# A linear-attention layer and its feed-forward net on one core: w_in fetched for two weight groups at a time

## The chip, the core and the metric

The kernel runs on one core of a Trainium2 chip. A core has a matrix engine (TensorE, PE in the profile), which also loads its stationary operands (PEld), a vector engine (VectorE, DVE), a scalar engine (ScalarE, ACT), a general one (GpSimd, POOL) and SyncE (SP), which here does nothing but issue transfers. Each engine works through its own list of instructions in a fixed order and waits at semaphores. Sixteen DMA engines move data between the memory of the chip and the 128 partitions of the on-chip buffer. The metric is the device time of one execution in microseconds (us).

## What is computed

```python
def _attn_ref(r, k, v, w, u):          # r, k, v, w: (4, 8, 768, 48), u: (8, 48)
    state = zeros((B, H, D, D))
    for t in range(S):
        cur = einsum('bhd,bhe->bhde', u[None] * k[:, :, t], v[:, :, t])
        y[:, :, t] = einsum('bhd,bhde->bhe', r[:, :, t], state + cur)
        state = w[:, :, t, :, None] * state + einsum('bhd,bhe->bhde', k[:, :, t], v[:, :, t])

def _moe_ref(x, w_in, w_out):          # x: (3072, 384), w_in: (384, 2048), w_out: (2048, 384)
    h = maximum(x @ w_in, 0.0)
    return (h * h @ w_out).astype(float32)
```

The attention's output, laid out as 3072 tokens of 384 channels, is the x of the feed-forward net. The inputs r, k, v, w and u are 4-byte floats. The weights w_in and w_out come as 8-byte floats, so a row of w_in has 16 KB and a row of w_out 3 KB.

## The kernel before

**Tiling.** The sequence of 768 steps is cut into six chunks of 128. Chunk c of sequence b (four sequences) is one attention unit; its output goes, transposed, into the tile x, 128 tokens of each sequence, so that a chunk gives the feed-forward net 512 tokens. That net runs over 16 blocks f of 128 hidden channels: `first` (L569, matmuls of L573) makes the block's hidden values in a PSUM tile hp, lines 578 to 582 on ACT and DVE apply the squared relu and split it into a rounded part and a rest (tile g), and `second` (L585, matmuls of L588) adds the block's share to the output tile ob. For the first chunk the blocks f 0 to 5 are done in halves of two sequences each (`HALF`, L605), 12 half blocks; from f = 6 on a block takes all 512 tokens.

**Weights.** They lie in eight groups g; group g holds the blocks 2g and 2g + 1. `load_w` (L298) issues for each group four transfers of w_in into the tile ri (for each half j of the partitions one of 48 partitions with three pieces of 2 KB each, 288 KB, and one of 16 partitions with three pieces, 96 KB; L305) and one of w_out into ro (768 KB, L307). In w_in a piece is 256 channels of 8 bytes out of a row of 16 KB. `split_w` (L310) then turns each group's w_in, and each group's w_out, into two 4-byte parts: on ACT a widening read into a buffer q (L318), on DVE three passes over q (L322, L326, L331), on ACT the rounded part (L338), on POOL the rest (L339). There are two buffers q. The results wi and wo lie where the raw data lay.

**Attention loads.** For chunk 1 and later, w, k and r of two sequences go by three transfers into a tile st (L358); DVE transposes blocks of it (L367); 16 transfers on chip spread these into the tile pt (L377); then the scans (L411) begin.

**Order.** The order of all instructions is written down before the program runs, by the class Plan. Every step is added with an engine, a cost, a rank and what it reads and writes. `order` (L75) keeps a clock for each engine and repeatedly takes, over all engines, the step that can start first; among those that can start at the same time on an engine, the one of lowest rank. For SP it models the transfers: at most eight in flight (`LANES`, L46, and the program waits likewise: each transfer waits for the semaphore of the eighth before it), a limit on the pieces outstanding (`RUNS`), and a result counts as there some time after the data has passed (`SLACK`). The ranks that matter here, from the tables of L598 to L604: a group's loads have W0[g] + WL[g], which is -20.75, -17.5, -10, -5.25, -1.5, -1.5, -3.25 and 3.5 for the groups 0 to 7; its splits have W0[g], -12.5, -9.5, -1, 0.25, 0.25, 5.5, 5.0 and 17. The st loads of chunk 1, first two sequences, have -7.25 and the 16 spreads after them -5.25. ro of group 6 shares its place with small tiles of chunk 0 and can be loaded only after these are read (L299); ri of group 7 likewise waits for a tile of the first loads.

So SP issues, in this order, ri and ro of the groups 0 and 1 among the loads of chunk 0; ri and ro of group 2; st of chunk 1 (three transfers); ri and ro of group 3; ri of group 6; ri of group 4; the 16 spreads; ro of groups 6 and 4; ri and ro of group 5; a v; ri and ro of group 7.

Of the kernel before, what the change touches and what calls it, by code (L numbers as in the profile page):

```python
# [10 lines left out]
F32R = mybir.dt.float32r  # L11
U8 = mybir.dt.uint8
U32 = mybir.dt.uint32
# [156 lines left out]

@with_exitstack
def kernel(
    ctx: ExitStack,
# [18 lines left out]
    R = 2 * D  # L194
    J = 64
    HP = J + D
    NF = DF // 128
    KT = DM // 128
    NG = NF // 2


    placed = {}

    def place(name, shape, dtype, at):
        n = 1
# [18 lines left out]
    for i in range(3):  # L224
        g = place(f"g{i}", [128, 2, 512], F32R, None)
# [11 lines left out]
    far = const.tile([128, NC * B], F32, name="far")  # L237
# [17 lines left out]
    P = Plan()  # L255
# [34 lines left out]
    w_in32 = w_in.bitcast(U32).rearrange("r (g x) -> g r x", g=NG)  # L290
    w_out32 = w_out.bitcast(U32).rearrange("(g f p) x -> g p f x", p=128, f=2)
    wi = {2 * g + f: wi_t[g].rearrange("p z (k f x) -> p z k f x", k=KT, f=2)[:, :, :, f] for g in range(NG) for f in range(2)}
    wo = {2 * g + f: wo_t[g][:, :, f * DM:f * DM + DM] for g in range(NG) for f in range(2)}

    def first_use(n):
        return [s for s in P.steps if both[n]["st"] in s.slots]

    def load_w(g, rank):  # L298
        before = first_use(0) if g == NG - 1 else [s for s in P.steps if any(x.pool == "ly" for x in s.slots)] if g == NG - 2 else []  # L299

        pairs = w_in32[g, 0:KT * R].rearrange("(k p) x -> p k x", k=KT)
        for j in range(2):
            last = w_in32[g, KT * R + j * D:KT * R + j * D + D].rearrange("(k p) x -> p k x", k=KT)
            for i, (to, n, src) in enumerate(((j * J, D, pairs[j * D:j * D + D]), (j * J + D, J - D, last))):
                P.add("sp", 1.4 if n == D else 0.5, rank, lambda to=to, n=n, src=src: nc.sync.dma_start(out=wi_r[g][to:to + n], in_=src),  # L305
                      w=[("wi", g, j, i)], after=before if g == NG - 1 else [], runs=3 * n)
        P.add("sp", 2.4, rank, lambda: nc.sync.dma_start(out=wo_r[g], in_=w_out32[g]), w=[("wo", g, 0, 0)],  # L307
              after=before, runs=256)

    def split_w(g, rank):  # L310
        for nm, rt, tt, parts in (("wi", wi_r[g], wi_t[g], [("wi", g, j, i) for j in range(2) for i in range(2)]),
                                  ("wo", wo_r[g], wo_t[g], [("wo", g, 0, 0)])):
            bits = rt.rearrange("p k x -> p (k x)").rearrange("p (x z) -> p x z", z=2)
            q = Slot("q")
            raw, lead = (nm, g, "raw"), (nm, g, "lead")

            def widen(q=q, bits=bits):
                A.activation(q.tile, bits.bitcast(F32)[:, :, 1], AF.Copy, scale=2.0 ** -112)  # L318
# [19 lines left out]
            P.add("act", 0.74, rank, lambda q=q, tt=tt: A.copy(out=tt[:, 0], in_=q.tile), r=[q], w=parts + [lead])  # L338
            P.add("pool", 1.9, rank, lambda q=q, tt=tt: G.tensor_tensor(out=tt[:, 1], in0=q.tile, in1=tt[:, 0].bitcast(F32), op=ALU.subtract),  # L339
                  r=[q, lead], w=[(nm, g, "rest")])  # L340
# [257 lines left out]
    AT = {"load": -12.5, "z": -10, "pt": -10.5, "rk": -7.0, "beta": -5.0, "far": 9.25, "v": -6.0, "scan": -2.25, "ln": 7.0, "rt": -6, "kn": 3.25, "diag": -3.5, "mt": 5, "mask": 3.25, "ktp": 5.25, "kt": 12.5, "mix": 4.25, "x": 1.5, "x3": -5.0, "send": 3.0, "dS": 3.5, "S": 1.25}  # L598
    AT0 = {"load": -13.0, "turn": -1.5, "rk": -2, "beta": 0.2, "far": 9.25, "v": -6.75, "scan": -1.75, "ln": 5.25, "rt": 0.25, "kn": 2, "diag": 9.5, "mt": -1.0, "mask": 3.75, "ktp": 7.25, "kt": -1, "mix": 3, "x": 7.75, "x3": -1, "send": 4.0, "dS": 7.5, "S": -4}
    U0 = (-16, -15.25, -6.75, -5.5)  # L600
    C1 = (5.25, 13, 34.5, 36)
    WL = (-8.25, -8, -9, -5.5, -1.75, -7, -8.25, -13.5)
    OFF = {"hp": -1.0, "g": -6.5, "ob": 0.75, "os": -7.5}
    W0 = (-12.5, -9.5, -1, 0.25, 0.25, 5.5, 5.0, 17)  # L604
    HALF = (6, 16, 0, 0, 0, 0)  # L605
    LAG = 2

    def rank_of(c, b):
        if c == 0:
            return lambda nm: U0[b] + AT0[nm]  # L610
        return lambda nm: (C1[b] if c == 1 else 8 * ((c - 1) * B + b) - 4) + AT[nm]

    for b in range(B):
        attention(0, b, rank_of(0, b))
    for g in range(NG):
        load_w(g, W0[g] + WL[g])
        split_w(g, W0[g])
    x = 0
    for c in range(NC):
        if c:  # L620
            for b in range(B):
                attention(c, b, rank_of(c, b))

        order = [(f, bs) for bs in ((0, 2), (2, B)) for f in range(HALF[c])] + [(f, (0, B)) for f in range(HALF[c], NF)]
        for f, bs in order:
            step = (bs[1] - bs[0]) / 2
            ffn(P, c, f, lambda nm, x=x, step=step: x + OFF[nm] + (LAG * step if nm in ("ob", "os") else 0), bs)
            x += step
    with tc.manual_schedule():
        P.run()  # L630
# [14 lines left out]
    with tc.If(any_bad > 0):  # L645
        with tc.tile_pool(name="dram", bufs=1, space=bass.MemoryType.DRAM) as dr, \
# [8 lines left out]
            with tc.For_i(0, S, TB) as t0:  # L655
# [8 lines left out]
                for t in range(TB):  # L664
                    rt, kt, wt = (tk[nm][:, t].unsqueeze(2).broadcast_to(sh) for nm in "rkw")
# [7 lines left out]
                for b in range(B):  # L673
                    nc.sync.dma_start(
                        out=xd[b * S:b * S + S].rearrange("s (h d) -> h s d", d=D)[:, ds(t0, TB)],
                        in_=ys[b * H:b * H + H])
            with tc.For_i(0, S, C) as s0:
# [17 lines left out]
                P = Plan()  # L695
# [36 lines left out]
```

## Time and profile before

| | |
|---|---|
| time, median of 3 runs | 560.74 us (558.96 to 561.72) |
| span of the profiled execution | 559.9 us |
| PE busy | 530.8 us, 95% of the span |
| DVE busy | 359.1 us, 64% |
| ACT busy | 288.0 us, 51% |
| POOL busy | 101.3 us, 18% |
| transfers issued from SP (q1) | 49.17 MB, 43.9% of 16 engines |
| w_in transfers of 288 KB, 16 of them, median to landing | 9.1 us |
| w_in transfers of 96 KB, 16 of them | 8.1 us |
| w_out transfers of 768 KB, 8 of them | 9.6 us |

Shares of busy time are over the whole span. The span has two parts: about 110 us in which the weights arrive and are split while the first two chunks run, and the rest, in which only PE has no idle time. The page gives no own time for the profiled execution beside its span; the median of the runs is 0.8 us above the span.

### The profile page before, as it was taken

The page shows a single profiled execution, that of the slowest core. Times are in us where ns is not written, and L with a number is a line of the kernel's source. Part 1 is how long each engine was busy: PE and PEld are TensorE (multiplying, and loading weights), DVE is VectorE, ACT ScalarE, POOL GpSimd, SP SyncE. Part 2 cuts the span into 40 slices and gives each one's busy share as a digit, 9 for nine tenths or more (in the row PEclk, how much of TensorE's full clock was granted, in tenths as well). Part 3 has the DMA queues.
Part 4 walks back from the last instruction along what each step waited for, and adds up shares of the span by engine and source line. Part 5 has one row for each costly group of instructions (what it writes and reads, how often), then busy time and mean ns, then how long its engine had stood idle before and what let it go on. Part 6 is the DMA issues. An engine that isn't in the chain of part 4 may idle for free. (4 is left out here: it accounts for less than half of the span.)

```text
span 559.9 us, 10076 instructions
## 1 busy us (share of the span) xinstructions
PE 530.8 (95%) x3800; PEld 466.7 (83%) x3800; DVE 359.1 (64%) x643; ACT 288.0 (51%) x677; POOL 101.3 (18%) x115
## 2 busy tenths in 40 slices
PE   4768898999999999999999999999999999999995
PEld 3557787889998999988888888888888888998994
DVE  5789879898759596776866767567475233332330
ACT  2786776668554747555554554553563222332322
POOL 4253552352203003030401102102000000000000
PEclk9998898999999999999999999999999999999999
DMA  9999699237472645637470470460440000010001
GB/s 156 210 240 217 122 255 218 39 64 137 99 141 51 111 109 91 123 78 135 80 132 2 78 168 24 84 129 2 78 106 3 12 1 1 14 58 2 0 1 60
DMA packets 206326, 50.86 MB, mean 91 GB/s; under 512 B 196032, under 2 KB 201152, under 8 KB 206272
## 3 DMA queue, kind: packets, MB, share of 16 engines
q1 hardware_dynamic: 205552, 49.17, 43.9%
q10 hardware_dynamic: 720, 0.98, 0.5%
q8 instruction: 32, 0.52, 0.4%
q14 instruction: 22, 0.18, 0.1%
HBM read 31.65 MB, written 4.72 MB: 65 GB/s over the span
## 5 line engine op out<-in xcount | busy, mean ns | idle before, releaser
L573 PE MATMUL hp<-x,wi 128*128 128x512 f32 (+1 forms) x1062 | 225.6, 358 | 4.7 <-DVE g L582 4.7
L588 PE MATMUL ob<-wo,g 128*128 128x384 f32 x1152 | 224.7, 341 | 4.4 <-ACT g L581 4.4
L588 PEld LDWEIGHTS ob<-wo,g 128*128 128x128 f32 x1152 | 200.5, 189 | 12.2 <-ACT g L581 4.9
L573 PEld LDWEIGHTS hp<-x,wi 128*128 128x128 f32 x1062 | 175.5, 190 | 31.9 <-DVE g L582 5.8
L579 DVE SCALAR_TENSOR_TENSOR hp<-hp,t 128x512 f32<-128x512 f32 (+1 forms) x118 | 70.2, 596 | 110.5 <-ACT t L578 110.0
L578 ACT ACTIVATE t<-hp 128x512 f32<-128x512 f32 (+1 forms) x118 | 60.9, 516 | 136.8 <-PE hp L573 111.2
L582 DVE TENSOR_TENSOR g<-hp,g 128x512 fp32r<-128x512 f32 (+1 forms) x118 | 69.1, 586 | 37.7 <-ACT g L581 35.9
L581 ACT CAST g<-hp 128x512 fp32r<-128x512 f32 (+1 forms) x118 | 59.2, 504 | 54.6 <-DVE hp L579 54.4
L448 ACT ACTIVATE m<-ident,beta 128x128 f32<-128x128 f32 x192 | 60.5, 395 | 7.0 <-DVE beta L441 7.0
L438 POOL TENSOR_TENSOR st<-st 128x384 f32<-128x384 f32 x24 | 25.1, 1047 | 64.7 <-DVE st L367 63.5
L463 DVE COPY_PREDICATED m<-caus,a 128x512 f32<-128x512 uint8 x48 | 33.0, 731 | 5.5 <-PE a L459 5.5
L459 PEld LDWEIGHTS a<-pt 48*128 48x128 f32 x384 | 25.8, 199 | 11.4 <-issue 7.1
L459 PE MATMUL a<-pt 48*128 48x128 f32 x384 | 30.8, 298 | 4.4 <-DVE pt L431 4.4
L526 DVE SCALAR_TENSOR_TENSOR x<-a,x 112x128 fp32r<-112x128 f32 (+2 forms) x44 | 17.9, 432 | 20.5 <-ACT x L525 19.9
L493 PE MATMUL a<-m,v 128*48 128x128 f32 (+1 forms) x384 | 28.5, 291 | 2.3 <-DVE m L463 1.8
L525 ACT ACTIVATE x<-a 112x128 fp32r<-112x128 f32 (+2 forms) x44 | 15.2, 389 | 28.8 <-PE a L493 28.5
L411 DVE TENSOR_TENSOR_SCAN pt<-pt,zero 112x128 f32<-112x128 f32 x80 | 28.9, 410 | 0.3 <-DMA x<-x 0.3
L493 PEld LDWEIGHTS a<-m,v 128*48 128x48 f32 (+1 forms) x384 | 21.4, 134 | 7.5 <-issue 4.5
L440 POOL TENSOR_TENSOR st<-st,un 128x384 f32<-128x384 f32 x24 | 26.9, 1120 | 1.6
L367 DVE STREAM_TRANSPOSE st<-st 128x1152 f32<-128x1152 f32 x20 | 26.8, 1359 | 0.0
L553 POOL TENSOR_TENSOR S<-S,Ec 112x192 f32<-112x192 f32 x16 | 8.2, 510 | 102.0 <-DVE S L552 102.0
L418 ACT ACTIVATE m<-pt 112x512 f32<-112x512 f32 x24 | 15.2, 635 | 20.1 <-DVE pt L411 15.7
(72 smaller groups left out, 394.5 us busy)
## 6 DMA issues: line engine op xcount, KB each, us to landing
pt<-st SPq DMA_DIRECT2D x80, 96.0 KB, 2.3
ro<-in_moe_w_out_dram SPq DMA_DIRECT2D x8, 768.0 KB, 9.6
v<-in_v_dram SPq DMA_DIRECT2D x24, 192.0 KB, 3.1
ri<-in_moe_w_in_dram SPq DMA_DIRECT2D x16, 288.0 KB, 9.1
st<-in_w_dram SPq DMA_DIRECT2D x11, 384.0 KB, 4.7
st<-in_k_dram SPq DMA_DIRECT2D x11, 384.0 KB, 5.3
st<-in_r_dram SPq DMA_DIRECT2D x11, 384.0 KB, 5.6
pt<-st SPq DMA_DIRECT2D x80, 48.0 KB, 2.5
```

What stands on the lines that cost most here:

```text
L411: lambda p=p: V.tensor_tensor_scan(out=pt[:, 0, p], data0=src(0)[:, p], data1=zero.broadcast_to([HP, C]), initial=1.0, op0=ALU.mult, op1=A ...
L440: P.add("pool", 1.0, rank("rk"), lambda: G.tensor_tensor(out=rk(), in0=rk(), in1=un.rearrange("s (h d) -> s h d", d=D), op=ALU.mult), w=[( ...
L448: A.activation(mv(j)[:, p], ident, AF.Copy, scale=beta.tile[:, 2 * p + j:2 * p + j + 1])
L459: T.matmul(mts[j].tile.rearrange("s (p t) -> s p t", p=NP)[:, p], pt[js, 2, p], pt[js, 1, p], start=True, stop=True)
L463: lambda j=j: V.copy_predicated(out=mv(j), mask=caus.unsqueeze(1).broadcast_to([128, NP, C]), data=mts[j].tile.rearrange("s (p t) -> s p t ...
L493: T.matmul(ybv()[j * J:j * J + n_, p], vt.tile[:, o:o + n_], mv(j)[:, p], start=(c == 0 and p == KT), stop=True, skip_group_check=True)
L573: T.matmul(hp.tile[:, 0:n], wi[f][:, wl, kt], xT[:, kt, xl, xs], start=(m == 0), stop=(m == 3 * KT - 1))
L578: P.add("act", 0.5 if full else 0.28, rank("g"), lambda: A.activation(t(), h(), AF.Relu), r=[hp], w=[(g, 1)])
L579: P.add("dve", 0.61 if full else 0.33, rank("g"), lambda: V.scalar_tensor_tensor(out=h(), in0=h(), scalar=0.0, in1=t(), op0=ALU.max, op1=A ...
L581: P.add("act", 0.53 if full else 0.31, rank("g"), lambda: A.copy(out=hi(), in_=h()), r=[hp], w=[(g, 0)])
L582: P.add("dve", 0.61 if full else 0.33, rank("g"), lambda: V.tensor_tensor(out=lo(), in0=h(), in1=hi().bitcast(F32), op=ALU.subtract), r=[h ...
L588: T.matmul(obs[b][:, 0:DM], g.tile[0][:, gl, o:o + C], wo[f][:, wl], start=(f == 0 and m == 0), stop=(f == NF - 1 and m == 2))
```

## The change

The tables of ranks move from the function into a class Ranks with the same numbers. For the groups 2 and 3, and for 4 and 5, the raw w_in now lies in one tile of two groups, and the loads of the first group of the pair fetch both: for each half j of the partitions and each of the three row blocks z one transfer of 48 partitions, in which a partition gets the 2 KB pieces of two neighbouring groups. In memory these are 4 KB side by side; on the chip they go to two places 6 KB apart. The transfers of 16 partitions stay one per group. `load_w` of the second group of a pair issues only its w_out. The pair's loads have the rank of its first group, so -10 and -1.5. `split_w` of a paired group waits for four kinds of transfer (three z and the one of 16 partitions) in place of two. In the planner a transfer of 288 KB cost 1.4; each new one costs 0.93.

```diff
-    for g in range(NG):
-        wi_r.append(place(f"ri{g}", [128, KT, 512], U32, None))
-        wi_t.append(place(f"wi{g}", [128, 2, 2 * DM], F32R, placed[f"ri{g}"]))
-        wo_r.append(place(f"ro{g}", [128, 2, 2 * DM], U32, None))
-        wo_t.append(place(f"wo{g}", [128, 2, 2 * DM], F32R, placed[f"ro{g}"]))
+    both_r = {}
+    for gs in ((0,), (1,), (2, 3), (4, 5), (6,), (7,)):
+        raw = place(f"ri{gs[0]}", [128, len(gs), KT, 512], U32, None)
+        if len(gs) == 2:
+            both_r[gs[0]] = raw
+        for z, g in enumerate(gs):
+            wi_r.append(raw[:, z])
+            wi_t.append(place(f"wi{g}", [128, 2, 2 * DM], F32R, placed[f"ri{gs[0]}"] + 4 * KT * 512 * z))
...
+        if g in both_r:
+            two = w_in32[g:g + 2]
+            pairs = two[:, 0:KT * R].rearrange("g (k p) x -> p k g x", k=KT)
+            for j in range(2):
+                last = two[:, KT * R + j * D:KT * R + j * D + D].rearrange("g (k p) x -> p k g x", k=KT)
+                for z in range(KT):
+                    P.add("sp", 0.93, rank, lambda j=j, z=z, pairs=pairs: nc.sync.dma_start(out=both_r[g][j * J:j * J + D, :, z], in_=pairs[j * D:j * D + D, z]),
+                          w=[("wi", g, j, z), ("wi", g + 1, j, z)], runs=2 * D)
+                for z in range(2):
+                    P.add("sp", 0.5, rank, lambda j=j, z=z, last=last: nc.sync.dma_start(out=both_r[g][j * J + D:j * J + J, z], in_=last[:, :, z]),
+                          w=[("wi", g + z, j, KT)], runs=KT * (J - D))
         pairs = w_in32[g, 0:KT * R].rearrange("(k p) x -> p k x", k=KT)
-        for j in range(2):
+        for j in range(0 if g in both_r or g - 1 in both_r else 2):
...
-        for nm, rt, tt, parts in (("wi", wi_r[g], wi_t[g], [("wi", g, j, i) for j in range(2) for i in range(2)]),
+        for nm, rt, tt, parts in (("wi", wi_r[g], wi_t[g], [("wi", g, j, i) for j in range(2) for i in range(KT + 1 if g in both_r or g - 1 in both_r else 2)]),
```

More of the change, by code (lines that the diff above doesn't have):

```diff
@@ L168, in run, with unit, load, split @@
             s.fn()
+class Ranks:
+    AT = {'load': -12.5, 'z': -10, 'pt': -10.5, 'rk': -7.0, 'beta': -5.0, 'far': 9.25, 'v': -6.0, 'scan': -2.25, 'ln': 7.0, 'rt': -6, 'kn': 3.25, 'diag': -3.5, 'mt': 5, 'mask': 3.25, 'ktp': 5.25, 'kt': 12.5, 'mix': 4.25, 'x': 1.5, 'x3': -5.0, 'send': 3.0, 'dS': 3.5, 'S': 1.25}
+    AT0 = {'load': -13.0, 'turn': -1.5, 'rk': -2, 'beta': 0.2, 'far': 9.25, 'v': -6.75, 'scan': -1.75, 'ln': 5.25, 'rt': 0.25, 'kn': 2, 'diag': 9.5, 'mt': -1.0, 'mask': 3.75, 'ktp': 7.25, 'kt': -1, 'mix': 3, 'x': 7.75, 'x3': -1, 'send': 4.0, 'dS': 7.5, 'S': -4}
+    AT1 = {'load': -12.5, 'z': -10, 'pt': -10.5, 'rk': -7.0, 'beta': -5.0, 'far': 9.25, 'v': -6.0, 'scan': -2.25, 'ln': 7.0, 'rt': -6, 'kn': 3.25, 'diag': -3.5, 'mt': 5, 'mask': 3.25, 'ktp': 5.25, 'kt': 12.5, 'mix': 4.25, 'x': 1.5, 'x3': -5.0, 'send': 3.0, 'dS': 3.5, 'S': 1.25}
+    U0 = (-16, -15.25, -6.75, -5.5)
+    C1 = (5.25, 13, 34.5, 36)
+    W0 = (-12.5, -9.5, -1, 0.25, 0.25, 5.5, 5.0, 17)
+    WL = (-8.25, -8, -9, -5.5, -1.75, -7, -8.25, -13.5)
+    OFF = {'hp': -1.0, 'g': -6.5, 'ob': 0.75, 'os': -7.5}
+    LAG = 2
+    def unit(self, c, b, name):
+        if c == 0:
+            return self.U0[b] + self.AT0[name]
+        if c == 1:
+            return self.C1[b] + self.AT1[name]
+        return 32 * (c - 1) + 8 * b - 4 + self.AT[name]
+    def load(self, g):
+        return self.W0[g] + self.WL[g]
+    def split(self, g):
+        return self.W0[g]
+    def ffn(self, name, x, step):
+        return x + self.OFF[name] + (self.LAG * step if name in ("ob", "os") else 0)
+RANKS = Ranks()
+HALF = (6, 16, 0, 0, 0, 0)
 @with_exitstack
@@ L213 @@
     wi_r, wi_t, wo_r, wo_t = [], [], [], []
-    for g in range(NG):
-        wi_r.append(place(f"ri{g}", [128, KT, 512], U32, None))
-        wi_t.append(place(f"wi{g}", [128, 2, 2 * DM], F32R, placed[f"ri{g}"]))
-        wo_r.append(place(f"ro{g}", [128, 2, 2 * DM], U32, None))
-        wo_t.append(place(f"wo{g}", [128, 2, 2 * DM], F32R, placed[f"ro{g}"]))
+    both_r = {}
[6 more added lines that the diff above has]
+            wi_t.append(place(f"wi{g}", [128, 2, 2 * DM], F32R, placed[f"ri{gs[0]}"] + 4 * KT * 512 * z))
+        for g in gs:
+            wo_r.append(place(f"ro{g}", [128, 2, 2 * DM], U32, None))
+            wo_t.append(place(f"wo{g}", [128, 2, 2 * DM], F32R, placed[f"ro{g}"]))
     sel = place("sel", [HP, KT, J], F32, placed[f"ro{NG - 2}"])
@@ L595, in ffn @@
                 P.add(q_, 1.1, rank("os"), lambda b=b, os_=os_, ob=ob, e=e: e.dma_start(out=ob[c * C:c * C + C] if s0 is None else ob[ds(s0, C)], in_=os_.tile[:, 0:DM]), r=[os_])
[L598 to L611, printed above, removed]
     for b in range(B):
-        attention(0, b, rank_of(0, b))
+        attention(0, b, lambda nm, b=b: RANKS.unit(0, b, nm))
     for g in range(NG):
-        load_w(g, W0[g] + WL[g])
-        split_w(g, W0[g])
+        load_w(g, RANKS.load(g))
+        split_w(g, RANKS.split(g))
     x = 0
@@ L621 @@
             for b in range(B):
-                attention(c, b, rank_of(c, b))
+                attention(c, b, lambda nm, c=c, b=b: RANKS.unit(c, b, nm))
         order = [(f, bs) for bs in ((0, 2), (2, B)) for f in range(HALF[c])] + [(f, (0, B)) for f in range(HALF[c], NF)]
@@ L626 @@
             step = (bs[1] - bs[0]) / 2
-            ffn(P, c, f, lambda nm, x=x, step=step: x + OFF[nm] + (LAG * step if nm in ("ob", "os") else 0), bs)
+            ffn(P, c, f, lambda nm, x=x, step=step: RANKS.ffn(nm, x, step), bs)
             x += step
```

## The prediction

> **What bounds the kernel now.** I read the page first, then engine time by stretches, then the waits of the first part, then the queues.
>
> ```profile
> span 559.9 us, 10076 instructions
> ...
> PE   4768898999999999999999999999999999999995
> ...
> DMA  9999699237472645637470470460440000010001
> ```
>
> PE is full from the eighth slice (14 us each) on; the transfers are full only in the first five. In the stretches the columns are the stretch, its length, and the busy time of PE, PEld, DVE, ACT and POOL, then PE's granted clock, DMA share and GB/s:
>
> ```profile
> 28.00:42.00 14.00, 9.63 (x108) 8.37 (x104) 11.92 (x24) 11.61 (x28) 7.44 (x8) 1.00 1.05 239
> 42.00:56.00 14.00, 11.56 (x84) 10.04 (x86) 13.00 (x22) 8.76 (x22) 4.40 (x3) 0.87 1.04 217
> 56.00:70.00 14.00, 12.37 (x129) 10.84 (x127) 11.21 (x21) 10.21 (x27) 7.66 (x6) 0.88 0.66 122
> 70.00:84.00 14.00, 12.95 (x81) 12.15 (x81) 10.87 (x22) 10.19 (x27) 7.05 (x4) 1.00 0.97 255
> 84.00:98.00 14.00, 11.98 (x52) 9.83 (x50) 13.41 (x21) 8.81 (x14) 3.60 (x2) 0.88 1.03 218
> ...
> 112.00:553.00 441.00, 441.00 (x3146) 390.86 (x3146) 268.48 (x483) 213.96 (x512) 55.94 (x68) 1.00 0.34 67
> ```
>
> From 112 us on PE never stops, so a change in weight loads can win or lose only before. Between 28 and 98 us PE is idle for 4.37 + 2.44 + 1.63 + 1.05 + 2.02 = 11.5 us, and a clock of 0.87, 0.88 and 0.88 over 14 us costs 1.8 + 1.7 + 1.7 = 5.2 us. Those 16.7 us are all there is to win behind 28 us; before it, loads of chunk 0 that stand ahead of any changed transfer set the pace. What ends PE's idle time there? The waits between 28 and 112 us, and the same for readers of w_in's raw tile:
>
> ```profile
> POOL wo L339 <- ACT wo L338: 26.0, 7, 8.1
> POOL wi L339 <- ACT wi L338: 13.2, 4, 6.6
> ...
> PE hp L573 <- DVE g L582: 4.7, 3, 2.0
> ...
> PE ob L588 <- ACT g L581: 4.4, 1, 4.4
> ```
> ```profile
> L318 ACT ACTIVATE q<-ri x8: 889/896/939, 18.2 to 107.7; 128x768 f32<-128x768 f32 x8
> ...
> its engine sat idle before it (us, times) until:
>   POOL wi L339: 0.9, 1
> ...
> DMA to landing us min/median/max: 4.6/8.8/13.2
> ```
>
> The first reader of a w_in tile never stood waiting for its transfer; its only idle time, 0.9 us, was ended by POOL. PE waits for DVE and ACT, which work through splits, masks and relu in their written order (DVE 13.00 and 13.41 of 14 us in the stretches with the larger clock losses). **The bound of the front is that order, not the w_in transfers.**
>
> **The change part by part.** The rank tables keep their numbers: 0 us.
>
> *Reading speed.* Two stretches in which hardly anything else moved, the first w_in alone, the second w_out nearly alone:
>
> ```profile
> 54.00:60.00 6.00, 5.36 (x56) 4.02 (x56) 4.93 (x6) 2.44 (x5) 5.22 (x4) 0.72 1.05 197
> ...
> 74.00:76.00 2.00, 1.03 (x6) 0.71 (x5) 1.82 (x4) 2.00 (x7) 1.09 (x1) 1.00 0.98 369
> ```
>
> w_in in 2 KB pieces goes at 197 GB/s; w_out, in 3 KB rows that follow one another, at 369, both with the engines full. A pair has 2 x (3 x 192 + 2 x 96) KB = 1.57 MB: 8.0 us at the one rate, 4.3 at the other. So reading 4 KB side by side is worth 0 to 3.7 us of transfer time per pair, 7.4 in all, and could fall below 0 only by the overhead of four more transfers, below. I take 0 (the pieces still land as 2 KB, the row nearest), but neither end reaches the sum: since no reader waits for ri, what hides a gain is the same written order that hides the transfer now. Without that cover it would be the 7.4 us.
>
> *Issue.* A pair has ten w_in transfers instead of eight, four more in all. SP's queue (start, length, line, what, count):
>
> ```profile
> 34.77 0.44 SPq L358 DMA_DIRECT2D st<-in_w_dram  x1
> 36.25 5.38 SPq L358 DMA_DIRECT2D st<-in_k_dram  x1
> 41.68 1.39 SPq L358 DMA_DIRECT2D st<-in_r_dram  x1
> 43.11 4.17 SPq L305 DMA_DIRECT2D ri<-in_moe_w_in_dram  x4
> 47.33 0.43 SPq L307 DMA_DIRECT2D ro<-in_moe_w_out_dram  x1
> 47.80 10.68 SPq L305 DMA_DIRECT2D ri<-in_moe_w_in_dram  x8
> ...
> 59.67 12.03 SPq L377 DMA_DIRECT2D pt<-st  x16
> 71.81 1.11 SPq L307 DMA_DIRECT2D ro<-in_moe_w_out_dram  x2
> 72.97 2.10 SPq L305 DMA_DIRECT2D ri<-in_moe_w_in_dram  x4
> 75.11 0.60 SPq L307 DMA_DIRECT2D ro<-in_moe_w_out_dram  x1
> ```
>
> Unhindered, one w_in issue takes 2.10 / 4 = 0.52 us, so four are 2.1 us of SP. They hide: the eight of 47.80 took 10.68 us for 4.2 us of issuing, SP waiting for transfers in flight. 0 us; 2.1 at most.
>
> [...]
>
> *What moves in SP's queue.* The rows above are, by rank, st of chunk 1, ri and ro of group 3, ri of groups 6 and 4, the spreads, ro of 6 and 4, and group 5. Group 3's w_in now goes with group 2's, at rank -10, ahead of ro of group 2 and of the st loads of chunk 1. That is 0.79 MB, 4.0 us at 197 GB/s, by which these come later. Is there room? The three st transfers' own view, then DVE in order of time:
>
> ```profile
> DMA to landing us min/median/max: 8.4/8.7/8.9
> ```
> ```profile
> 54.92 2.61 DVE L367 STREAM_TRANSPOSE st<-st 128x1152 f32<-128x1152 f32 x2
> ```
>
> The last st (41.68) lands by 41.68 + 8.9 = 50.6 and is read at 54.92; plus 4.0 it lands at 54.6. It just fits: 0 us, and at the other end, if the planner allows its usual margin on top, these transposes and the spreads behind them go back by up to 4 us. Group 3's split, earlier in data, gains nothing: both buffers q are taken until POOL is done with group 2.
>
> The second pair is the delicate move. Ahead of the spreads at 59.67 now stand group 6 and group 4, 1.57 MB. With the first pair's bytes moved forward and the start of the spreads bound to the transposes, about the same bytes fit, which is group 6 and roughly half of the pair 4 and 5. Once the spreads are ready, their rank (-5.25) beats the pair's (-1.5), and ro of group 6 (-3.25) does too. So the tail of the pair, with the last parts of group 4, goes where group 5 goes now, at 72.97 to 75.1. Group 4, then, counts as landed at about 73.7 + 8.8 = 82.5 (four transfers behind the spreads, the median to landing). It is needed here (the fifth widening on ACT in order of rank; POOL's end of it; PE, where after 12 half blocks and f = 6 and 7 the blocks f = 8 and 9 start at 86.70 and 93.08):
>
> ```profile
> 73.21 0.90 ACT L318 ACTIVATE q<-ri 128x768 f32<-128x768 f32 x1
> ```
> ```profile
> 79.14 1.85 POOL L339 TENSOR_TENSOR wi<-q,wi 128x768 fp32r<-128x768 f32 x1 [1.76 <-ACT wi L338]
> ```
> ```profile
> 86.70 2.26 PE L573 MATMUL hp<-x,wi 128*128 128x512 f32 x9
> 88.81 2.25 PE L588 MATMUL ob<-wo,g 128*128 128x384 f32 x12
> 93.08 3.91 PE L573 MATMUL hp<-x,wi 128*128 128x512 f32 x9 [2.02 <-DVE g L582]
> 96.82 1.21 PE L588 MATMUL ob<-wo,g 128*128 128x384 f32 x6
> ```
>
> From widening to the finished rest it takes 79.14 + 1.85 - 73.21 = 7.8 us, so f = 8 could start at 82.5 + 7.8 = 90.3 instead of 86.70: 3.6 us late. What stands in that time is 2.26 us of PE; the twelve ob matmuls of 88.81 can go before it, and the hole before 93.08 takes some of it. Its ob share is not due before 96.82. The splitting engines, meanwhile, can do group 6, long landed, in group 4's place, and group 4 when they now do group 6: the same DVE work in another order. So the cost lies between -2.0 (the hole of 2.02 us fills) and +3.6; I take +0.3, near the middle of what filling leaves.
>
> **The sum.** Ranks 0, reading 0, issue 0, st 0, order +0.3: a span of 559.9 + 0.3 = 560.2, and 0.8 us for the step from this span to the median of the runs (560.74): **561.0 us**, no change that can be measured; a measurement of this kernel tells about 0.5%, 2.8 us, from none.
>
> **Rivals.**
> *Group 4 is late and PE stands (slower).* One mechanism: the tail of the second pair behind the 16 spreads. It decides from a landing later than 86.70 - 7.8 = 78.9. For it speaks the queue above; against it, group 6 to work on. If the ob work does not fill, PE loses 3.6 us, and the clock row says what follows a hole: nine matmuls of 128x512 took 2.26 us at 86.70 and 3.91 behind the hole of 2.02 us, 1.65 more. 3.6 + 1.65 = 5.3: 566.0 us.
> *The new order closes a hole (faster).* The hole before 93.08 and its slow clock are worth 2.02 + 1.65 = 3.7 us; it follows splits of two tiles done side by side on DVE, which another order separates. 560.7 - 3.7 = 557.0 us. Against it: DVE is at 13.41 of 14 us there.
> *It does not do what it says.* Each piece still lands as 2 KB; if memory was not what held the 197 GB/s, the pairs read as slowly as before, and only the order changes: 561.0 us as well.
>
> **How the numbers follow.** Forecast 0.42 and no faster reading 0.08, both within 0.5%; slower by the late group 0.29; faster by a closed hole 0.21. The range reaches from 556.5, just beyond the closed hole, to 566.5, just beyond the late group; 4 us on the spreads would be 565.0, inside. Some 0.09 is left out on either side, with the full 7.4 us of reading (553.6) below. The likeliest case's own range is 558.0 to 563.5.
>
> **What would show it.** Right: w_in's raw tile still without idle time ended by a transfer; the st loads of chunk 1 issued 3 to 4 us later than 34.77; a few transfers of the pair behind the spreads; group 4 widened at 82 or later, with f = 8 starting near 90; PE full from about 112 us. Reading speed: the rate while a pair moves, near 197 or near 369 GB/s. Wrong: PE idle between 28 and 112 us off from 11.5 by over 3 us, or any added hole behind 112 us, which would mean that the new order reaches beyond the weights.

## The result, and the profile after

| | before | after |
|---|---|---|
| time, median | 560.96 us (558.29 to 562.84, 20 runs) | 563.14 us (559.95 to 567.38, 20 runs) |
| ratio | | 1.0052 (95%: 1.0036 to 1.0068) |
| a later comparison on one chip | 560.60 us (20 runs) | 564.88 us (8 runs), 1.0079 (1.0043 to 1.0114) |
| span of the profiled execution | 559.9 us | 563.2 us |

The change makes the kernel slower by half a per cent or a little more. (The ratios here are estimated from all runs, not from the two medians; these lie 0.39% apart.) The profiled execution of the changed kernel took 565.05 us at a mean clock of 0.981, while the median of its 20 runs is 563.14 us at 0.987, so its trace shows more half clock than most of its runs have.

The lines of the class Plan keep their place; those of `load_w` and `split_w` stand 40 to 51 lines further down (widening L318 is now L369, the rounded part L389, the rest L390, the w_out transfer L307 is L358), the hidden block's matmuls L573 are L624, and L588 is L639. Of the attention, the st loads L358 are L409, the transposes L367 are L418 and the spreads L377 are L428.

First the page, then the engines by stretches (columns as before: stretch, length, busy time of PE, PEld, DVE, ACT and POOL, PE's clock, DMA share, GB/s):

```profile
span 563.2 us, 10088 instructions
...
DMA packets 206390, 50.86 MB, mean 90 GB/s; under 512 B 196096, under 2 KB 201216, under 8 KB 206336
```
```profile
28.00:42.00 14.00, 9.29 (x99) 8.20 (x98) 12.04 (x25) 12.03 (x31) 8.08 (x8) 0.95 1.11 211
42.00:56.00 14.00, 12.39 (x58) 10.93 (x59) 11.40 (x18) 7.41 (x18) 2.81 (x3) 0.62 1.02 234
56.00:70.00 14.00, 12.77 (x132) 10.34 (x129) 8.91 (x15) 5.89 (x13) 7.38 (x6) 0.70 0.89 163
70.00:84.00 14.00, 13.86 (x94) 13.17 (x93) 12.23 (x25) 12.97 (x37) 4.39 (x3) 1.00 0.76 125
84.00:98.00 14.00, 12.59 (x61) 10.49 (x59) 12.60 (x21) 8.48 (x16) 6.10 (x4) 1.00 1.06 262
98.00:112.00 14.00, 12.41 (x104) 10.19 (x105) 13.73 (x23) 9.13 (x15) 6.50 (x6) 1.00 0.54 102
...
140.00:154.00 14.00, 12.62 (x133) 11.26 (x133) 10.60 (x21) 8.81 (x29) 4.49 (x5) 1.00 0.46 103
154.00:556.00 402.00, 402.00 (x2832) 356.04 (x2831) 232.73 (x424) 187.79 (x440) 40.84 (x53) 1.00 0.32 64
```

The packets from 2 KB to under 8 KB are 206336 - 201216 = 5120, as many as before (206272 - 201152): the pairs land in the same 2 KB pieces. Between 28 and 112 us PE is idle for 4.71 + 1.61 + 1.23 + 0.14 + 1.41 + 1.59 = 10.7 us, 0.8 less than before, when 98 to 112 us was full. But the clock of 0.62 and 0.70 in two stretches, and 0.95 in one, costs 5.3 + 4.2 + 0.7 = 10.2 us where it cost 5.2. And 1.4 us of PE's time is idle between 140 and 154 us, where before none was. Together this is 5.6 us more than before; not all of it reaches the end (the spans differ by 3.3 us). Which part does not is not shown; a slow clock ahead of a wait that would come anyway is the likely one.

Was a transfer waited for? The view of w_in's raw tile, then SP's queue, of the changed kernel:

```profile
L369 ACT ACTIVATE q<-ri x8: 887/916/923, 18.0 to 107.5; 128x768 f32<-128x768 f32 x8
...
its engine sat idle before it (us, times) until:
who waited for it (us, times):
```
```profile
34.39 3.31 SPq L347 DMA_DIRECT2D ri<-in_moe_w_in_dram  x3
37.97 1.21 SPq L350 DMA_DIRECT2D ri<-in_moe_w_in_dram  x2
39.43 0.39 SPq L358 DMA_DIRECT2D ro<-in_moe_w_out_dram  x1
41.52 0.39 SPq L409 DMA_DIRECT2D st<-in_w_dram  x1
...
53.10 1.42 SPq L347 DMA_DIRECT2D ri<-in_moe_w_in_dram  x3
58.35 1.75 SPq L350 DMA_DIRECT2D ri<-in_moe_w_in_dram  x2
64.00 0.39 SPq L358 DMA_DIRECT2D ro<-in_moe_w_out_dram  x1
64.49 12.88 SPq L428 DMA_DIRECT2D pt<-st  x16
77.41 1.61 SPq L347 DMA_DIRECT2D ri<-in_moe_w_in_dram  x3
79.06 1.18 SPq L350 DMA_DIRECT2D ri<-in_moe_w_in_dram  x2
```

Under "sat idle before it" nothing is named: no reader stood waiting for w_in. What moved is the order. The first pair (L347 is its 48-partition transfers, L350 those of 16; the first rows shown are its second half) is issued until 39.2 us; w_out of group 2 follows it, and st of chunk 1 comes at 41.52 where it came at 34.77. The second half of the pair 4 and 5 stands behind the 16 spreads, at 77.41; its last transfers land at about 85.5 us.

What follows from that on the engines, in order of time. The first fence has group 2 before (its widening on ACT and its first matmuls on PE); then after: ACT's widening of groups 2 and 4, DVE's transposes of chunk 1, and PE:

```profile
43.23 0.94 ACT L318 ACTIVATE q<-ri 128x768 f32<-128x768 f32 x1
...
60.19 1.33 PE L573 MATMUL hp<-x,wi 128*128 128x256 f32 x9
```
```profile
48.74 0.92 ACT L369 ACTIVATE q<-ri 128x768 f32<-128x768 f32 x1
...
89.78 0.91 ACT L369 ACTIVATE q<-ri 128x768 f32<-128x768 f32 x1
```
```profile
61.06 2.63 DVE L418 STREAM_TRANSPOSE st<-st 128x1152 f32<-128x1152 f32 x2
```
```profile
58.15 1.30 PE L544 MATMUL a<-m,v 128*64 128x128 f32 x8 [0.81 <-DVE m L514]
59.37 1.55 PE L559 MATMUL a<-ly,sel 48*64 48x128 f32 x12
...
63.77 1.15 PE L544 MATMUL a<-m,v 128*48 128x128 f32 x12
64.85 2.40 PE L624 MATMUL hp<-x,wi 128*128 128x256 f32 x18
...
94.20 2.73 PE L624 MATMUL hp<-x,wi 128*128 128x512 f32 x11
98.19 1.89 PE L624 MATMUL hp<-x,wi 128*128 128x512 f32 x7 [1.25 <-POOL wi L390]
```

Group 2 was widened at 43.23 before and is at 48.74 now; its first hp came at 60.19 and comes at 64.85. So from 58 to 65 us PE has the small matmuls of the attention alone, and the clock from 56 to 70 us is 0.70. Group 4, widened at 73.21 before, is at 89.78, some 4 us after its data landed: ACT has other work first in its written order. Of the 11 matmuls at 94.20 the last two, from 96.31 on, are the first of f = 8, the first block of group 4; the third needs the group's unfinished rest, and PE stands 1.25 us, until 98.19.

### The profile page after: what moved, and what is told of

Its sections match the earlier page's. It is cut to its first block, busy times and chain, and to the rows that moved or that the text cites. A ratio compares the mean times of both kernels' runs of the same rounds, so it can differ in the third digit from the quotient of the medians.

```text
span 563.2 us, 10088 instructions
## 1 busy us (share of the span) xinstructions
PE 534.5 (95%) x3800; PEld 469.4 (83%) x3800; DVE 358.2 (64%) x643; ACT 288.3 (51%) x677; POOL 99.7 (18%) x115
## 2 busy tenths in 40 slices
DMA packets 206390, 50.86 MB, mean 90 GB/s; under 512 B 196096, under 2 KB 201216, under 8 KB 206336
## 5 line engine op out<-in xcount | busy, mean ns | idle before, releaser
L639 PE MATMUL ob<-wo,g 128*128 128x384 f32 x1152 | 225.6, 341 | 6.0 <-ACT g L632 5.7
L624 PE MATMUL hp<-x,wi 128*128 128x512 f32 (+1 forms) x1062 | 224.6, 358 | 2.1 <-POOL wi L390 1.3
L639 PEld LDWEIGHTS ob<-wo,g 128*128 128x128 f32 x1152 | 201.1, 189 | 14.2 <-ACT g L632 6.6
L624 PEld LDWEIGHTS hp<-x,wi 128*128 128x128 f32 x1062 | 175.3, 191 | 29.4 <-POOL wi L390 1.7
L510 PEld LDWEIGHTS a<-pt 48*128 48x128 f32 x384 | 27.7, 209 | 12.2 <-issue 8.3
L510 PE MATMUL a<-pt 48*128 48x128 f32 x384 | 33.1, 310 | 4.3 <-DVE pt L482 4.3
L462 DVE TENSOR_TENSOR_SCAN pt<-pt,zero 112x128 f32<-112x128 f32 x80 | 30.2, 421 | 0.0
L418 DVE STREAM_TRANSPOSE st<-st 128x1152 f32<-128x1152 f32 x20 | 26.8, 1358 | 0.0
L390 POOL TENSOR_TENSOR wi<-q,wi 128x768 fp32r<-128x768 f32 x8 | 15.9, 1991 | 50.4 <-ACT wi L389 50.4
```

Of the source, the lines that this page charges most:

```text
L418: V.transpose(out=zt[:, i].rearrange("a t p q i -> a t (p q) i"), in_=sv[:, :, i].rearrange("s t p q x -> s t (p q) x"))
L462: lambda p=p: V.tensor_tensor_scan(out=pt[:, 0, p], data0=src(0)[:, p], data1=zero.broadcast_to([HP, C]), initial=1.0, op0=ALU.mult, op1=A ...
L510: T.matmul(mts[j].tile.rearrange("s (p t) -> s p t", p=NP)[:, p], pt[js, 2, p], pt[js, 1, p], start=True, stop=True)
L624: T.matmul(hp.tile[:, 0:n], wi[f][:, wl, kt], xT[:, kt, xl, xs], start=(m == 0), stop=(m == 3 * KT - 1))
L639: T.matmul(obs[b][:, 0:DM], g.tile[0][:, gl, o:o + C], wo[f][:, wl], start=(f == 0 and m == 0), stop=(f == NF - 1 and m == 2))
```

## The experiments

Theories: the new written order costs the time (as a whole; by the late group 2; by the late group 4); the pairs are read more slowly; the clock alone does it. All ratios are to the kernel before on the same chip.

**e0_before**: the kernel before, unchanged, to see how far two sets of runs of one kernel lie apart.

> The kernel before, unchanged, for its own trace and the granted clock of each of its runs. Theory 'order' (the loss of 2 to 3 us comes from the new written order of PE, DVE and ACT between 40 and 65 us, through stretches at half clock): the mean granted clock of its runs is higher than the changed kernel's (median 0.987 over 20 runs, 0.963 to 0.996), 0.989 or more. Theory 'reading' (the pairs' pieces come in more slowly, and that is what costs): the clock need not differ. Theory 'chance' (the profiled execution of the changed kernel was only an unlucky one): the clocks of both spread alike.

561.21 against 561.26 us, ratio 1.0001 (0.998 to 1.0022). A difference of 0.5% is more than this comparison makes by itself.

**e1_pairs_old_order**: the pairs' transfers under the order of before. The steps of each group stay in the plan at their places and with their costs; the first group's steps issue the pair's three 48-partition transfers, those of the second issue none:

```diff
+            def fetch_two(j=j):
+                two = w_in32[g:g + 2, 0:KT * R].rearrange("g (k p) x -> p k g x", k=KT)
+                for z in range(KT):
+                    nc.sync.dma_start(out=both_r[g][j * J:j * J + D, :, z], in_=two[j * D:j * D + D, z])
...
+                fetch = lambda to=to, n=n, src=src: nc.sync.dma_start(out=wi_r[g][to:to + n], in_=src)
+                if first is not None and n == D:
+                    fetch = fetch_two if g == first else lambda: None
-                P.add("sp", 1.4 if n == D else 0.5, rank, lambda to=to, n=n, src=src: nc.sync.dma_start(out=wi_r[g][to:to + n], in_=src),
+                P.add("sp", 1.4 if n == D else 0.5, rank, fetch,
```

> Transfers of the changed kernel (pairs), in the written order of the kernel before on PE, DVE, ACT and POOL. 'Order': 560.9 us, as before (ratio 0.998 to 1.002). 'Reading': 563 us, as after (ratio 1.004 to 1.007). The reading rate while a pair moves is near 165 GB/s here too.

567.39 us, 1.012 (1.0092 to 1.0147): slower than the change itself. The waits of ACT between 28 and 112 us, and PE in order of time:

```profile
ACT wi L354 <- DMA ri<-in_moe_w_in_dram: 7.4, 1, 7.4
```
```profile
87.13 3.64 PE L589 MATMUL hp<-x,wi 128*128 128x512 f32 x9 [6.27 <-DVE g L598]
```

ACT waits 7.4 us for a transfer before it may write the rounded part of group 4, although group 4 was widened at 73.49 and its own data was there by then. The pair lies in one tile, and group 5's 16-partition transfers still stand behind the spreads (issued at 77.61), so the wait seems to be on the tile as a whole. PE then stands 6.27 us. Neither forecast came true (561 or 563 us): the kernel says something about a shared tile, and what a hole at this place costs (6.1 us in all), but not yet about reading in pairs.

The changed kernel has the same shared tiles. There ACT's writes of the rounded part follow DVE's last pass over the same buffer by 0.08 us, so no transfer holds them up. For group 2 ("issue" says that the profile names no releaser; in group 4's case the pass ends at 94.52 and the write starts at 94.60):

```profile
53.97 0.94 DVE L382 SCALAR_TENSOR_TENSOR q<-ri,q 128x768 uint32<-128x768 uint32 x1
...
54.99 0.83 ACT L389 CAST wi<-q 128x768 fp32r<-128x768 f32 x1 [4.25 <-issue]
```

**e4_pairs_old_order_together** mends this: all ten transfers of a pair at the first group's place, the order of the four engines as before.

```diff
-                if first is not None and n == D:
-                    fetch = fetch_two if g == first else lambda: None
+                if first is not None:
+                    fetch = (fetch_two if n == D else lambda j=j: last_two(j)) if g == first else lambda: None
```

> Pairs in the written order of the kernel before, as in e1, but all ten transfers of a pair go out at its first group's place, so that no part of group 5 follows the spreads. In e1 ACT's cast into group 4's place stood 7.4 us for a transfer of w_in. 'Shared tile' (that cast waits for every transfer into the pair's tile, also those of the other group): the 6.27 us hole of PE at 81 us goes and the time is 561 to 563 us. 'Reading' (the pairs come in too slowly for the old order): the hole stays in part, 565 us or more.

561.97 us, 1.0027 (0.9999 to 1.0055). The hole of 6.27 us is gone, which confirms the reading of e1. Reading in pairs by itself lies within 0.6% of the kernel before, and cannot be told from no change; but the interval also reaches the change's own 0.52%, so that this kernel alone does not clear the pairs. The next one does.

**e2_singles_new_order**: the reverse. The written order of after on all engines, but in the pairs' places each group's 48-partition rows are fetched by themselves with three pieces for a partition, as before (into the shared tile of the change).

```diff
-                    P.add("sp", 0.93, rank, lambda j=j, z=z, pairs=pairs: nc.sync.dma_start(out=both_r[g][j * J:j * J + D, :, z], in_=pairs[j * D:j * D + D, z]),
+                    def fetch(j=j, z=z):
+                        if z < 2:
+                            nc.sync.dma_start(out=both_r[g][j * J:j * J + D, z], in_=two[z, 0:KT * R].rearrange("(k p) x -> p k x", k=KT)[j * D:j * D + D])
+                    P.add("sp", 0.93, rank, fetch,
```

> The written order of the changed kernel on PE, DVE, ACT and POOL, with the transfers of the kernel before (one group each, three pieces of 2 KB per partition) in the pairs' places. 'Order': 563 us, as after (ratio 1.004 to 1.007). 'Reading': 561 us, as before (ratio 0.998 to 1.002), at a reading rate near 197 GB/s.

564.52 us, 1.0070 (1.0045 to 1.0095). Its engines by stretches repeat those of after:

```profile
42.00:56.00 14.00, 12.38 (x62) 10.88 (x63) 10.85 (x18) 6.86 (x16) 2.80 (x2) 0.62 1.00 222
56.00:70.00 14.00, 12.79 (x130) 10.35 (x129) 9.43 (x16) 5.90 (x13) 6.86 (x6) 0.72 0.90 180
```

The loss is there without any transfer of two groups. It comes with the order.

**e3_pairs_apart**: as after, but the second of a pair's two pieces begins 4 KB behind the first, so that there are 2 KB between them and the two are not side by side (the groups 3 and 5 then hold other columns of w_in than theirs).

```diff
-            pairs = two[:, 0:KT * R].rearrange("g (k p) x -> p k g x", k=KT)
+            pairs = w_in32[g:g + 4].rearrange("(a b) r x -> b a r x", b=2)[0][:, 0:KT * R].rearrange("g (k p) x -> p k g x", k=KT)
```

> The changed kernel, but a pair transfer fetches the pieces of groups g and g + 2 instead of g and g + 1: the same transfers, with 2 KB between the two pieces instead of none. The blocks 4 to 11 then use other columns of w_in, so the values differ. 'Order': 563 us, as after. 'Reading': if it is the neighbourhood of the two pieces that slows them, the rate goes back to about 197 GB/s and the time to 561 us; if it is the form of the transfer, both stay.

563.32 us, 1.0068 (1.0041 to 1.0095): that the pieces lie side by side in memory makes no difference that can be seen.

**e5_after_warm and e6_before_warm**: the kernel after, and the kernel before, with matmuls of the identity put into those holes of PE between 28 and 112 us that the planner foresees.

```diff
+        pe = [s for s in steps if s.engine == "pe"]
+        holes = {s: max(0.0, n.at - s.at - s.cost) for s, n in zip(pe, pe[1:])}
...
+            if warm and 28 < s.at < 112 and holes.get(s, 0.0) > 0.4:
+                for _ in range(int(0.85 * holes[s] / 0.15)):
+                    warm()
...
-        P.run()
+        P.run(lambda: T.matmul(obs[0][:, DM:DM + 128], ident, ident, start=False, stop=True, skip_group_check=True))
```

> The changed kernel with matmuls of the identity, into columns that nothing reads, put into PE's list behind the steps after which the planner foresees a hole between 28 and 112 us (85% of each hole). 'Clock' (the loss is the half clock between 43 and 64 us, kept low by an order in which PE has holes): the half clock behind 28 us shrinks from 20 us to under 10 and the time falls by 2 to 5 us, to 558 to 561. 'Holes' (the order itself costs the time): 563 us or more, the half clock changes nothing.

> The same matmuls of the identity in the kernel before. 'Clock': its 7 to 10 us at half clock behind 28 us shrink, 1.5 to 4 us less, 557 to 560 us, and the distance to e5_after_warm is smaller than 2.2 us, the distance of the two kernels. 'Holes': 561 us or more, the distance stays.

After with filled holes: 564.48 us, 1.0058 (1.0037 to 1.008). Before with filled holes: 560.41 us, 0.9988 (0.997 to 1.0006). The same stretch of the first:

```profile
42.00:56.00 14.00, 14.00 (x126) 13.52 (x125) 12.72 (x21) 7.67 (x19) 4.06 (x3) 1.00 1.04 246
```

The clock is full, and 4.1 us stay between the two. So raising the low clock of after does not remove its loss. The clock looks like a form that the loss takes: with a full clock the same lateness shows as PE without work. Counted from the trace's records, those of the identity left out, PE has no matmul for 18.9 us between the first hp and the last ob in e5, and for 15.8 us in e6; without the filling the two orders differed little in this (11.7 and 11.3 us), and much in the time at half clock (20.5 and 10.2 us).

**e7_reads**: only w_in's 48-partition transfers (the 16-partition ones and all computation are left out), each group followed by one pass of DVE that needs it. First single groups, then pairs side by side, pairs with a gap, rows of 4 KB, rows of 16 KB, then the first two again.

```python
def singles():
    for g in range(NG):
        pairs = wg[g, 0:KT * R].rearrange("(k p) x -> p k x", k=KT)
        for j in range(2):
            nc.sync.dma_start(out=raw[j * J:j * J + D, g], in_=pairs[j * D:j * D + D])
...
            for j in range(2):
                for z in range(KT):
                    nc.sync.dma_start(out=raw[j * J:j * J + D, at:at + 2, z], in_=two[j * D:j * D + D, z])
```

> No computation, only transfers of w_in, seven stretches of 4.7 MB with a pass of DVE over the tile between them: one group with three pieces of 2 KB per partition; pairs side by side; pairs with 2 KB between; rows of 4 KB to one place of 4 KB; whole rows of 16 KB; again the first and the second. If side by side helps the memory, the second has a higher rate than the first and the third. If the form of the transfer alone counts, second and third agree. If only longer pieces on the chip's side help, the fourth and the fifth are faster and the first three are near 200 GB/s.

DVE in order of time, single groups first, then pairs:

```profile
30.26 0.96 DVE L51 TENSOR_SCALAR raw<-raw 128x1536 uint32<-128x1536 uint32 x1 [1.75 <-DMA raw<-in_moe_w_in_dram]
32.96 0.96 DVE L51 TENSOR_SCALAR raw<-raw 128x1536 uint32<-128x1536 uint32 x1 [1.73 <-DMA raw<-in_moe_w_in_dram]
...
58.19 1.83 DVE L51 TENSOR_SCALAR raw<-raw 128x1536 uint32<-128x1536 uint32 x2 [4.55 <-DMA raw<-in_moe_w_in_dram]
64.72 1.83 DVE L51 TENSOR_SCALAR raw<-raw 128x1536 uint32<-128x1536 uint32 x2 [4.69 <-DMA raw<-in_moe_w_in_dram]
```

Every pass is released by a transfer, so the steps are the transfers' own time: 2.70 us for a group of 0.59 MB (218 GB/s), 6.53 us for a pair of 1.18 MB (181 GB/s), 1.1 us longer than two groups singly. With a gap between the pieces it is as slow; the stretches have 180 GB/s side by side and 181 apart:

```profile
40.00:66.00 26.00, 6.78 (x8) 0.00 (x0) 1.00 1.08 180
67.00:91.00 24.00, 5.53 (x7) 0.00 (x0) 1.00 1.08 181
```

The two repeats at the end of the same run agree in order (2.52 us for a group, 6.4 to 6.5 for a pair); it is one run. So pairs are read more slowly, but in the changed kernel no reader waits for them.

That left the question which part of the order costs. Two kernels take the two late groups apart, and the third repeats after on the same chip.

**e8_pairs_two_ranks**: after, with two ranks altered, so that group 6 gives way to the second pair. Group 2 is as late as in after, group 4 is not.

```diff
-    W0 = (-12.5, -9.5, -1, 0.25, 0.25, 5.5, 5.0, 17)
-    WL = (-8.25, -8, -9, -5.5, -1.75, -7, -8.25, -13.5)
+    W0 = (-12.5, -9.5, -1, 0.75, 0.25, 5.5, 5.0, 17)
+    WL = (-8.25, -8, -9, -5.5, -1.75, -7, -6.25, -13.5)
```

> The changed kernel with two numbers of its ranks altered: WL of group 6 from -8.25 to -6.25 (its loads asked for later) and W0 of group 3 from 0.25 to 0.75 (its split later). The pairs are read as in the changed kernel and group 2 is as late as there (its split near 48.7 us, hp of f=4 near 64.9), but the pair 4,5 goes ahead of the 16 spreads, so that group 4 is split near 70 instead of 89.8 and group 6 takes the late place. Theory 'late group 4': the time falls back to that of the kernel before, 561 +-1 (ratio 0.998 to 1.002), and PE's part without a matmul between 70 and 112 us falls under that of the changed kernel. Rival 'late group 2' (the front costs it): 563 to 564.5, as the changed kernel. Rival 'side by side is read slower': 563 or more too.

**e9_pair45_only**: only the groups 4 and 5 as a pair. Group 2 is as early as before, group 4 behind the spreads.

```diff
-    for gs in ((0,), (1,), (2, 3), (4, 5), (6,), (7,)):
+    for gs in ((0,), (1,), (2,), (3,), (4, 5), (6,), (7,)):
```

> The kernel before with only groups 4 and 5 as a pair; groups 2 and 3 are fetched singly as before. The front up to about 60 us stands as before (split of group 2 at 43.2, hp of f=4 near 60.2, columns st of chunk 1 near 34.8), and group 4 comes behind the spreads as in the changed kernel (split near 89 us). Theory 'late group 4': the whole loss stays, 563 to 564.5 (ratio 1.004 to 1.007). Rival 'late group 2': no loss, 561 +-1. Rival 'side by side is read slower': half of the loss, near 562.

> The changed kernel as it is, beside the two above on the same chip, so that they are compared with it directly: 563 to 564 (ratio 1.0036 to 1.0068 as measured before); split of group 2 near 48.7 and of group 4 near 89.8 us. Should it come out at 561 here, neither lateness has a price that can be measured on this chip.

On that chip, beside 560.60 us before: e8 562.46 us, 1.0039 (1.0017 to 1.0061); e9 565.77 us, 1.0108 (1.0078 to 1.0137); after again 564.88 us, 1.0079 (1.0043 to 1.0114). ACT's widenings of w_in and PE in e8:

```profile
48.41 0.92 ACT L369 ACTIVATE q<-ri 128x768 f32<-128x768 f32 x1
57.48 0.91 ACT L369 ACTIVATE q<-ri 128x768 f32<-128x768 f32 x1
71.50 0.90 ACT L369 ACTIVATE q<-ri 128x768 f32<-128x768 f32 x1
```
```profile
89.10 2.26 PE L624 MATMUL hp<-x,wi 128*128 128x512 f32 x9
93.29 2.26 PE L624 MATMUL hp<-x,wi 128*128 128x512 f32 x9
```

Group 2 is widened at 48.41, late as in after; group 4 at 71.50, earlier than before; f = 8 starts at 89.10 and nothing holds PE there. In e9 it is the other way round, group 2 at 42.98 and group 4 at 85.39, and the engines by stretches have this (PE first, DVE third), then two rows of PE:

```profile
84.00:98.00 14.00, 13.47 (x99) 11.35 (x98) 14.00 (x26) 7.92 (x14) 3.35 (x2) 1.00 1.03 228
98.00:112.00 14.00, 12.28 (x69) 9.68 (x68) 13.25 (x18) 8.85 (x13) 9.24 (x6) 1.00 0.31 61
112.00:126.00 14.00, 11.68 (x95) 8.99 (x94) 12.28 (x19) 8.19 (x20) 7.74 (x6) 0.88 0.51 90
```
```profile
115.25 1.21 PE L510 MATMUL a<-pt 48*128 48x128 f32 x16 [2.32 <-DVE pt L482]
116.44 3.82 PE L624 MATMUL hp<-x,wi 128*128 128x512 f32 x9
```

From 98 to 126 us, PE is idle for 4.0 us where before it was full, behind a DVE that is full from 84 to 98: the splits of the late groups meet the scans and masks of chunk 1. The blocks f = 8 and 9 of group 4 wait for no weights in e9 (PE's waits for a rest of w_in are 0.5 us up to 130 us, for the groups 5 and 7); PE stands for DVE's work on chunk 1, 2.32 us at 115.25, and the nine matmuls behind that hole take 3.82 us in place of 2.26.

So the second pair behind the spreads brings the whole loss without a late group 2. That a late group 2 is not needed is shown by this; what it costs by itself is not. e8 has it, and the pairs, with group 4 early: its median is 1.9 us above before where after's is 4.3, so more than half of the loss goes and some stays. That lies between what the two theories expected (561 and 563 or more), and e9 came out above its forecast of 563 to 564.5. The two kernels also move other splits than these two (e8 that of group 3), so the prices of the two parts are not exact, and they do not add up: e9 is 0.9 us above after.

**e11_two_ranks_warm**: e8 with the holes filled as in e5, to see what is left of its loss.

> The kernel with pairs and two altered ranks, with identity matmuls put into the holes of PE between 28 and 112 us that the planner foresees, as in the two kernels before that had them. Theory 'what is left of its loss (562.5 against 560.6) is half clock behind the holes at 37.9 to 56, since its runs granted 0.980 to 0.981 where those of the kernel before granted 0.989': the clock comes to about 0.998 and the time to 560.4 as the kernel before with such matmuls (ratio 0.997 to 1.000). Rival 'the late group 2 has a price of its own in idle PE': the time stays near 562.5 (ratio near 1.004) with the full clock. No version here is expected to beat the kernel before by more than 0.3%.

560.89 against 561.07 us, 1.0002 (0.9983 to 1.0021), at a clock of 0.999. Against e5 it differs in the two ranks and in the holes that follow from them; both have the full clock, and 1.0058 (1.0037 to 1.008) became 1.0002. That is the clearest pair of the study: **the change's loss lies in where its plan puts the second pair and the splits behind it.** By which of the waits it reaches the end is read from the traces, not tested one by one. What e8 still loses (1.0039) looks like half clock in the front, since it goes with filled holes (most of e8's runs have a mean clock of 0.98, those of before 0.989); the two intervals overlap slightly, so that part is likely and not shown. No version here beats the kernel before by more than its interval.

## Why the prediction came out as it did

561.0 us was predicted, 563.14 us measured: inside the range (556.5 to 566.5) and inside the likeliest case's own (558.0 to 563.5), but slower by 0.52%, just over the bound for no change, and the repeat with 0.79% is plainly over it. That the range holds the time is owed to its width: "no change that can be measured" did not come true. By its steps:

- *The bound of the front is the written order, not the w_in transfers*: right. No widening waited for w_in after the change, and the new order without pairs (e2) has the loss, while pairs without the new order (e4) have none that can be told from no change.
- *Reading speed 0*: as a term of the sum no run speaks against it, but its sign was wrong. Taken was 0, with 0 to 3.7 us of gain for a pair; e7 measured a loss of 1.1 us. The step compared single pieces of 2 KB with the rows of w_out and took the length of what is read side by side for the cause; e3 and e7 show that it is not. The cover held: no reader waited for the pairs. Why w_out's rows came at 369 GB/s stays open; they go to 128 partitions, the w_in transfers to 48.
- *Issue, four more transfers, 0*: nothing shows it as a cost. e4 has all of them, and its interval ends at 0.55%, 3.1 us; in e7 a pair, with two transfers more, took 1.1 us longer than two groups singly.
- *st of chunk 1 comes 4.0 us later and just fits*: it failed. It came 6.75 us later (41.52 for 34.77), the transposes 6.1 us (61.06 for 54.92) and the spreads 4.8 us (64.49 for 59.67). The other end that the prediction named, up to 4 us on the spreads, was nearer.
- *Not in the prediction at all*: half of the first pair's bytes are group 3's, so group 2's own w_in comes later too: its last transfer landed at about 45 us, before at about 40. The step named what stands behind the pair (w_out of group 2 and st), and not the pair's own first user. Group 2's widening went from 43.23 to 48.74 and its first hp from 60.19 to 64.85; the attention of chunk 0 is left alone on PE, at a low clock.
- *The tail of the second pair goes behind the spreads, group 6 takes group 4's place*: right, and seen in the queue. *Group 4 landed at 82.5, f = 8 at 90.3*: too early. The tail went out at 77.41 instead of 73, which the error in st, above, explains in part, and landed at about 85.5. But group 4 was widened only at 89.78: the step let the split start with the landing, and in the written order ACT had the split of group 6 and chunk 1's work first. So f = 8 began at 96.31 and stood at its third matmul.
- *Order +0.3 us*: this is the term that was mis-sized. Measured were +2.2 us (and +4.3 in the repeat). The price was taken near the middle of -2.0 and +3.6, on the ground that other work fills PE's time; it does fill part of it in after, where block f = 12 is pulled ahead of f = 8, but beside it stand the low clock of 42 to 70 us and the holes of 98 to 112 and 140 to 154 us. The rival *group 4 is late and PE stands*, at 566.0, named the right group, but had the path wrong: it let PE lose 3.6 us waiting for group 4's weights and 1.65 at a slow clock behind that. In after that wait was 1.25 us, at full clock, and in e9 there is none; what the late splits hold up there is DVE's work on chunk 1. That e9 has 565.77 us, close to 566.0, is luck.
- *What would show it*: "PE idle between 28 and 112 us off from 11.5 by over 3" did not happen (10.7), so the sign as chosen missed the loss: idle time gave way to time at a low clock. "Any added hole behind 112 us" did happen (1.4 us), and meant what it was said to mean.
- *A closed hole, 557.0*: the hole of 2.02 us before f = 9 did close, and other holes opened.

## What to carry to other kernels

When one transfer fetches for two users, list what the first user and everything queued behind it now wait for: half of the bytes ahead of them belong to someone who is not due yet. Where a planner writes the order, a changed transfer is a changed plan of every engine; take the two apart (the old order with the new transfers, the new order with the old transfers) before explaining a time by either. And count PE's idle time and its clock together: here one fell by 0.8 us while the other cost 5.0 us more.

## What the runs showed of the hardware

- In e7_reads 288 KB transfers with three 2 KB pieces for each partition, far apart in memory, moved w_in at 218 GB/s; 192 KB transfers with two such pieces side by side at 181 GB/s, and with a gap of 2 KB between the pieces as slowly. Longer contiguous rows were no faster: these are its stretches with rows of 4 KB and of 16 KB alone.

```profile
92.00:116.00 24.00, 4.81 (x6) 0.00 (x0) 1.00 1.02 173
118.00:141.00 23.00, 1.73 (x2) 0.00 (x0) 1.00 1.02 145
```

- The clock can be low without idle time to match. From 50 to 64 us in after, PE is busy for 12.91 of 14 us, mainly with matmuls of 48 rows or columns, its longest gap there is 0.81 us, and the clock over 42 to 56 and 56 to 70 us is 0.62 and 0.70. In this trace it changes in steps of 3.41 us: half for 6.83 us from 40.51, full for 3.41, half for 13.65. It fell at 50.75 us after a step in which PE was busy for 2.09 us (61%) with no gap over 1.33 us, stayed at half through steps with 3.13, 3.17 and 2.85 us busy, and came back at 64.40 after one without a gap. In e8 PE is busy for less of 42 to 56 us, 10.88 us where after has 12.39, at a clock of 0.88, so the busy share of a stretch alone does not say how low its clock is. Identity matmuls of 128 x 128 in the foreseen holes brought the clock to 1.00 there (e5), but no time that can be measured, neither in the order of after (1.0058) nor in that of before (0.9988); in the order of e8 they may have (1.0039 became 1.0002, the intervals overlapping slightly).
- In this program a wait can be on a whole tile where the data is in a part of it: 7.4 us, as far as the trace tells, on group 5's last transfers before a write into group 4's half (e1); with all transfers of the pair issued together the wait is gone (e4).
